# Attention output made transposed in 32-column tiles, beside the first feed-forward layer

## The chip, the core and the metric

The kernel runs on one core of a Trainium2 chip. The metric is the device time of one execution, in microseconds; the time of before is the median of 3 runs. The core's engines run unsynchronised programs and wait for each other through semaphores: PE (TensorE, the matmuls; PEld is its weight load), DVE (VectorE), ACT (ScalarE), POOL (GpSimd) and SP, which here only issues transfers.

## The reference, cut to what matters

Three things are computed one after the other: a linear attention with decay over 768 tokens (4 batches, 8 heads of 48), a gated layer of 384 -> 1536 -> 384 on all 3072 tokens, and a second layer of 384 -> 2048 -> 384.

```python
for t in range(S):                       # state: (B, H, D, D)
    kt, vt, rt = (k[:, :, t], v[:, :, t], r[:, :, t])
    cur = np.einsum('bhd,bhe->bhde', u[None] * kt, vt)
    y[:, :, t] = np.einsum('bhd,bhde->bhe', rt, state + cur)
    state = w[None, :, :, None] * state + np.einsum('bhd,bhe->bhde', kt, vt)
...
x = y as (3072, 384)
g = x @ w_gate;  x = (g * sigmoid(g) * (x @ w_val)) @ w_out
h = x @ w_in;    return (h * tanh(softplus(h))) @ w_out2
```

The term with `u` is a token's own: its output gets v times one number per head, the sum over the head of r·u·k. Below this number is called the own sum.

## The kernel before

**Tiling.** The tokens are cut into `NJ` = 6 blocks of 128; a block of 4 batches is 512 columns of the feed-forward layers. Inside a block the attention of one batch is a batch's "turns" on PE. The first layer runs in 72 units (block j, slice f of 128 of its 1536 features). A unit has 9 matmuls for the gate, 9 for the value and 9 for the previous unit's output ("out"): every product of 128x512 is three matmuls (`product`, L227 to L229), since each operand is split into a high part rounded to fp32r and the rest. ACT makes the silu (L614) and the high part of the product (`g_hi`, L620), DVE the product (L618) and the low part (`g_lo`, L626).

**Attention.** Blocks 0 and 1 (`EARLY` = 2) are done first, in the first 45 us. The attention of blocks 2 to 5 lies beside the units: the strings in `UNITS` give a unit's order and mark places ("fill"), and `Filler` hands the steps of `STEPS` out over these places. For a batch, PE has four turns: the scores k·r of 128 x 128 tokens (L444, 8 matmuls), the output as token x feature (L460 from the state, L468 from the masked scores, 24 matmuls with stationary tiles of 64 columns), three transposes of the output one place later (`at_flip`, L539), and the batch's addition to the state (L502, 8 matmuls; none in block 5). A plain fp32 matmul shows as two rows in the trace. Between them DVE masks the scores (L451, two of 128x512), adds the own term to the output (y, L489), takes the low part of the transposed output (L544), sums the state (L518) and makes the own sums (L425); ACT takes the high part (L540). POOL makes r·k (L417), times u (L419), own sum times v (L426), and puts the decay on r and k (L392, two of 128x512) and on the natural k (L434).

**Weights.** `Weights.tick` prepares one weight tile of 128x384 beside the units: ACT (L136), four DVE instructions on the bits (L144, L150, L158, L163), ACT again (L179) and one subtraction (`rest`, L185), on DVE for the first 36 tiles and on POOL after that. Units below 14 have two ticks, units 14 to 18 three in two units, 19 to 23 none, later units 1.3 each until all are done, at about 389 us. Every engine runs its instructions in program order, so a waiting instruction holds up all behind it.

Of the kernel before, what the change touches and what calls it, by code (L numbers as in the profile page):

```python
# [9 lines left out]
F32 = mybir.dt.float32  # L10
# [3 lines left out]
ALU = mybir.AluOpType  # L14
# [30 lines left out]
LAST = ["flip0", "low2"]  # L45

KEYS = [[(1, b, "mykeys0")] for b in range(B)]
STATES = [[(1, b, "state0" if i == 0 else "sum0")] for b in range(B) for i in range(2)]
NEXT = [[(1, B - 1, "own0 own1 decay1")], [(1, B - 1, "own2 decay0 keys0")]]
# [19 lines left out]
def tile_decay_attention_then_two_ffns(  # L69
    ctx: ExitStack,  # L70
    tc: tile.TileContext,
    rk_t: bass.AP,
    rkv_n: bass.AP,
    w_t: bass.AP,
    u_n: bass.AP,
    u_t: bass.AP,
# [181 lines left out]
    def at_tiles(j, b):  # L258

        if j < EARLY:  # L260
            r, k = (f32(wpool.tile([P, 2, DM], F32R, name="w_split")) for _ in range(2))
            r, k = (t.rearrange("p w n -> p (w n)")[:, : NPAIR * CH] for t in (r, k))
            r, k = (t.rearrange("p (n t) -> p n t", n=NPAIR) for t in (r, k))
            at_in[j, b] = {"r": r, "k": k}
        else:
            t = apool.tile([P, 2, NPAIR, CH], F32, name="rk_sb")
            n = apool.tile([P, 3, H, D], F32, name="n_sb")
            at_in[j, b] = {"r": t[:, 0], "k": t[:, 1], "both": t, "n": n}
            at_in[j, b].update({"av": n[:, 0], "kn": n[:, 1], "v": n[:, 2]})
# [5 lines left out]
    def load_at(j, b):  # L275
        a = at_in[j, b]
        if j < EARLY:
            nc.sync.dma_start(out=a["k"], in_=rk_t[j, b, :, 1])
            nc.sync.dma_start(out=a["r"], in_=rk_t[j, b, :, 0])
            nc.sync.dma_start(out=a["kv"], in_=rkv_n[j, b, :, 1:])  # L280
        else:
            nc.sync.dma_start(out=a["both"], in_=rk_t[j, b])
            nc.sync.dma_start(out=a["n"], in_=rkv_n[j, b])


    for b in range(B):
# [75 lines left out]
    late = apool.tile([P, 2, NPAIR, CH], F32, name="rk_sb")[:, 0]  # L362
    tabn = const.tile([P, H, D], F32, name="tabn")

    def tab_of_keys():
# [7 lines left out]
            tabn, ptab.rearrange("p n (i d) -> p (n i) d", d=PD)[:, :, 0:D], AF.Copy  # L373
        )

    mask3 = (
        mask.bitcast(mybir.dt.uint16).rearrange("p (o t) -> p o t", o=1).to_broadcast([P, NPAIR, CH])
    )


    state = const.tile([P, B, NPAIR, 2 * D], F32, name="state")
# [30 lines left out]
    def at_own(j, b, i):  # L412

        a = at_in[j, b]
        if i == 0:
            bonus[j, b] = epool.tile([P, DM], F32, name="pr").rearrange("p (h d) -> p h d", d=D)
            nc.gpsimd.tensor_tensor(out=bonus[j, b], in0=a["av"], in1=a["kn"], op=ALU.mult)  # L417
        elif i == 1:
            nc.gpsimd.tensor_tensor(  # L419
                out=bonus[j, b], in0=bonus[j, b], in1=u_sb.rearrange("p (h d) -> p h d", d=D),  # L420
                op=ALU.mult,
            )
        else:
            sums = epool.tile([P, H, 1], F32, name="bonus")
            nc.vector.reduce_sum(out=sums, in_=bonus.pop((j, b)), axis=AX.X)  # L425
            nc.gpsimd.tensor_tensor(  # L426
                out=a["av"], in0=a["v"], in1=sums.to_broadcast([P, H, D]), op=ALU.mult
            )

    def at_keys(j, b):  # L430
# [15 lines left out]
                    start=True, stop=True,  # L446
                )

    def at_mask(j, b):
        for g in range(2):  # L450
            nc.vector.copy_predicated(out=scores[g], mask=mask3, data=at[j, b]["scores"][g])  # L451

    def at_out(j, b):

        a = at[j, b]
        ps = a["out"] = ps_at.tile([P, 512], F32, name="at")
        if j:
# [15 lines left out]

    def at_mine(j, b):

        a = at[j, b]
        a["y"] = ypool.tile([P, DM], F32, name="y")
        nc.vector.tensor_tensor(
            out=a["y"].rearrange("p (h d) -> p h d", d=D), in0=a["v"],
            in1=a["sums"].rearrange("p (h o) -> p h o", o=1).to_broadcast([P, H, D]), op=ALU.mult,  # L480
        )

    def at_y(j, b):
        a = at[j, b]
        if j < EARLY:
            y = own = a["y"]
        else:
            y, own = ypool.tile([P, DM], F32, name="y"), a["av"].rearrange("p h d -> p (h d)")
        nc.vector.tensor_tensor(out=y, in0=a["out"][:, :DM], in1=own, op=ALU.add)  # L489
        a["y"] = y  # L490
# [60 lines left out]
    def after(j, b, n):  # L551
        n += j * B + b
        return order[n] if n < len(order) else None

    def at_part(j, b, part):

        nxt = after(j, b, 1)
        name, i = part[:-1], int(part[-1])
        if name == "scores":
            at_scores(j, b)  # L560
        elif name == "mask":
            at_mask(j, b)
        elif name == "out":
            at_out(j, b)
            at_fade(j, b)
        elif name == "y":
            at_y(j, b)
        elif name == "state":
            at_state(j, b)
        elif name == "sum":  # L570
            at_sum(j, b)
        elif name == "back" and b:
            at_flip(j, b - 1)
        elif name == "flip":
            at_flip(j, b)
        elif name == "low" and (i == 2 or i == 1 and b):
            at_low(j, b - (i == 1))
        elif name == "load":
            ahead = after(j, b, 2)
            if ahead:  # L580
                at_tiles(*ahead)
                load_at(*ahead)
        elif name == "own" and nxt:
            at_own(*nxt, i)
        elif name == "decay" and nxt:
            at_decay(*nxt, i)
        elif name == "keys" and nxt:
            at_keys(*nxt)
        elif name == "mykeys":
            at_keys(j, b)  # L590

    def at_steps(j):

        return [[(j, b, step)] for b in range(B) for step in STEPS + LAST * (b + 1 == B)]
# [223 lines left out]
    for f in range(NF1):  # L818
# [193 lines left out]
```

## Time and profile before

| what | value |
|---|---|
| median of 3 runs | 957.48 us (956.59 to 960.96) |
| span of the profiled execution | 955.2 us |
| PE busy | 944.3 us (99%) |
| PE weight load busy | 770.6 us (81%) |
| DVE busy | 628.2 us (66%) |
| ACT busy | 473.8 us (50%) |
| POOL busy | 163.5 us (17%) |
| granted clock of PE | full in all 40 slices |

The profiled execution's span lies 2.3 us below the median of the runs. Read it so: busy shares are means over the whole span, and what a stage waits for is read in its own stretch. A PE row lasts longer than the distance to the next row's start, since matmuls are pipelined; the distance between starts is what a matmul costs.

### The profile page before, as it was taken

The numbers are of one execution on the slowest core, as the hardware profiler recorded it, in microseconds if no ns is written. First come the engines' busy times: TensorE is split into PE (matmuls) and PEld (weight loads), VectorE is DVE, ScalarE is ACT, GpSimd is POOL, SyncE is SP. The second block draws the span as 40 slices with busy tenths as digits, with TensorE's granted clock in tenths as the row PEclk, the third lists the DMA queues.
The fourth block names the chain that finished last, engine by engine and source line by source line (L and its number), as shares of the span: only waits on it lengthen the run. The fifth ranks groups of instructions, "written<-read, shape, count | busy, mean of one in ns | idle before, by whom it ended". The sixth has DMA issues, their size and how long they took to land.

```text
span 955.2 us, 14700 instructions
## 1 busy us (share of the span) xinstructions
PE 944.3 (99%) x5707; PEld 770.6 (81%) x5707; DVE 628.2 (66%) x1170; ACT 473.8 (50%) x841; POOL 163.5 (17%) x148
## 2 busy tenths in 40 slices
PE   8999999999999999999999999999999999999998
PEld 6778888787788787888888888888888888888886
DVE  8998868446765766533322249868678777787774
ACT  2455543323343433311221248867676776777673
POOL 5100001764654464322000000000000000000000
PEclk9999999999999999999999999999999999999999
DMA  8464432446646655230046630001001010000000
GB/s 324 176 195 133 132 101 66 128 128 173 218 148 208 217 164 192 92 103 1 1 165 198 197 102 22 12 26 41 1 34 34 0 47 21 1 34 1 33 1 34
DMA packets 35781, 93.17 MB, mean 98 GB/s; under 512 B 4224, under 2 KB 4352, under 8 KB 35712
## 3 DMA queue, kind: packets, MB, share of 16 engines
q1 hardware_dynamic: 35280, 91.44, 29.5%
q0 software_dynamic: 432, 0.79, 0.6%
q8 instruction: 45, 0.74, 0.3%
q14 instruction: 24, 0.20, 0.1%
HBM read 69.41 MB, written 22.81 MB: 97 GB/s over the span
## 4 chain that ended last, share of the span: by engine, by line
PE 87%; DVE 5%; DMA 4%; issue 2%; ACT 1%; POOL 1%; SPq 0%; DVEq 0%; POOLq 0%; ACTq 0%
PE mm L227 12%; PE mm L228 11%; PE mm L229 11%; PE acc L227 11%; PE acc L228 11%; PE acc L229 11%; PE at L228 5%; PE at L229 4%; PE at L227 4%; DMA w_split<-rk_t 2%; PE at L468 2%; PE at L444 2%; PE at L460 1%; DVE w_num L150 1%; DVE w_num L144 1%
## 5 line engine op out<-in xcount | busy, mean ns | idle before, releaser
L227 PE MATMUL mm<-x_hi,w_split 128*128 128x512 f32 x546 | 217.6, 398 | 0.0
L229 PE MATMUL mm<-x_hi,w_split 128*128 128x512 f32 x546 | 213.0, 390 | 0.0
L228 PE MATMUL mm<-x_lo,w_split 128*128 128x512 f32 x546 | 212.9, 390 | 0.0
L228 PE MATMUL acc<-g_lo,w_split 128*128 128x512 f32 x483 | 188.4, 390 | 0.8 <-DVE g_lo L626 0.7
L227 PE MATMUL acc<-g_hi,w_split 128*128 128x512 f32 x483 | 188.8, 391 | 0.0
L229 PE MATMUL acc<-g_hi,w_split 128*128 128x512 f32 x483 | 188.0, 389 | 0.0
L618 DVE TENSOR_TENSOR o<-mm,o 128x512 f32<-128x512 f32 x72 | 49.7, 691 | 192.4 <-PE mm L229 162.4
L227 PEld LDWEIGHTS mm<-x_hi,w_split 128*128 128x128 f32 x546 | 102.5, 188 | 22.7 <-DVE o L618 0.4
L229 PEld LDWEIGHTS mm<-x_hi,w_split 128*128 128x128 f32 x546 | 102.5, 188 | 21.8
L228 PEld LDWEIGHTS mm<-x_lo,w_split 128*128 128x128 f32 x546 | 102.6, 188 | 20.0
L620 ACT ACTIVATE g_hi<-o 128x512 fp32r<-128x512 f32 x72 | 45.5, 632 | 141.4 <-DVE o L618 141.1
L228 PEld LDWEIGHTS acc<-g_lo,w_split 128*128 128x128 f32 x483 | 90.7, 188 | 21.0 <-DVE g_lo L626 2.0
L227 PEld LDWEIGHTS acc<-g_hi,w_split 128*128 128x128 f32 x483 | 90.6, 188 | 19.2
L229 PEld LDWEIGHTS acc<-g_hi,w_split 128*128 128x128 f32 x483 | 90.7, 188 | 18.8
L614 ACT ACTIVATE o<-mm 128x512 f32<-128x512 f32 x72 | 42.8, 594 | 89.5 <-PE mm L229 82.4
L848 ACT ACTIVATE e<-h 128x512 f32<-128x512 f32 x96 | 60.0, 626 | 53.4 <-DVE h L842 50.4
L855 ACT ACTIVATE e<-e 128x512 f32<-128x512 f32 x96 | 59.6, 621 | 49.4 <-DVE e L852 49.3
L862 DVE TENSOR_TENSOR h<-h,e 128x512 f32<-128x512 f32 x96 | 60.0, 687 | 20.5 <-ACT e L861 20.5
L185 POOL TENSOR_TENSOR w_raw<-w_num,w_raw 128x384 fp32r<-128x384 f32 x32 | 40.9, 1279 | 160.4 <-ACT w_raw L179 158.3
L227 PE MATMUL at<-x_hi,w_split 128*128 128x512 f32 x174 | 67.7, 389 | 0.0
L228 PE MATMUL at<-x_lo,w_split 128*128 128x512 f32 x174 | 67.7, 389 | 0.0
L229 PE MATMUL at<-x_hi,w_split 128*128 128x512 f32 x174 | 67.7, 389 | 0.0
(105 smaller groups left out, 1347.6 us busy)
## 6 DMA issues: line engine op xcount, KB each, us to landing
w_raw<-w SPq DMA_DIRECT2D x68, 384.0 KB, 3.5
w2s<-w_raw SPq DMA_DIRECT2D x32, 384.0 KB, 3.7
w_split<-w2s SPq DMA_DIRECT2D x32, 384.0 KB, 3.5
n_sb<-rkv_n SPq DMA_DIRECT2D x16, 576.0 KB, 4.9
rk_sb<-rk_t SPq DMA_DIRECT2D x16, 512.0 KB, 4.5
mid<-o SPq DMA_DIRECT2D x18, 256.0 KB, 2.2
rows<-mid SPq DMA_DIRECT2D x18, 256.0 KB, 2.6
y<-o SPq DMA_DIRECT2D x18, 256.0 KB, 2.3
```

The lines of the kernel that those rows point to most:

```text
L185: eng.tensor_tensor(out=t[:, 1, :], in0=num, in1=f32(t[:, 0, :]), op=ALU.subtract)
L227: nc.tensor.matmul(acc, lhsT=wt[:, 0, sl], rhs=hi, start=start, stop=False)
L228: nc.tensor.matmul(acc, lhsT=wt[:, 0, sl], rhs=lo, start=False, stop=False)
L229: nc.tensor.matmul(acc, lhsT=wt[:, 1, sl], rhs=hi, start=False, stop=stop)
L444: nc.tensor.matmul(ps[g][:, i, :], lhsT=a["k"][q, i, :], rhs=a["r"][q, i, :], start=True, stop=True,)
L468: nc.tensor.matmul(ps[t, h * D : (h + 1) * D], lhsT=scores[h % 2][:, h // 2, t], rhs=a["v"][:, h, :], start=(j == 0 and h == heads[0]), st ...
L614: nc.scalar.activation(sg, ps, AF.Silu)
L618: nc.vector.tensor_tensor(out=sg, in0=ps, in1=sg, op=ALU.mult)
L620: nc.scalar.activation(hi, sg, AF.Copy)
L848: nc.scalar.activation(es[n], hs[n], AF.Exp)
L855: nc.scalar.activation(e, e, AF.Ln, bias=1.0)
L862: nc.vector.tensor_tensor(out=hs[n], in0=hs[n], in1=es[n], op=ALU.mult)
```

## The change

**The output is made transposed.** For blocks 2 to 5 `at_turned` makes the output as feature x token at once: 28 fp32 matmuls per batch, each with a stationary tile of 32 columns (12 from the state, 16 from v) and 128 moving columns, consecutive ones on the column positions 0, 32, 64 and 96. `hi` (ACT) and `low` (DVE) read that PSUM tile. The transposes and the addition y are gone there. The own term enters as a diagonal: POOL writes the own sums on the diagonal of both score tiles (`at_diagonal`, two tensor_tensors of 128x512 over the identity), and the mask's copy then writes the scores beside it; L426 is gone.

**The steps are set anew.** A batch has two turns on PE: "out state" and "scores". POOL's steps are done two batches ahead. Block 2 begins one unit earlier, at unit 18, with its first steps (`AHEAD`, for its batches 0 and 1) put among the steps of units 14 to 17. For blocks 3 to 5 (`SPREAD`, 28 steps over 34 places) the mask of the even heads and that of the odd heads are two steps.

**A gate's low part in its own unit.** From unit 18 on `g_lo` is made by `mine`, behind the unit's own product, instead of `rest` in the next unit.

**Inputs.** r, k and v of a batch come by feature or in 32-column order in one transfer of 768 KB (`rkv_t`), and r and k by token in one of 384 KB, where there were 512 and 576 KB.

```diff
 STEPS = [
-    "scores0 own0", "mask0 back0 own1", "out0 low1 decay0 own2", "y0 state0 decay1 keys0",
-    "sum0 load0",
+    "out state load2 diag1", "hi low fade sum keys1", "scores1 first2 second2",
+    "mask1 total2 later2 sooner2",
+]
+SPREAD = [
+    "out state load2 diag1", "hi fade keys1", "low", "sum first2", "scores1 second2",
+    "even1 total2", "odd1 later2 sooner2",
 ]
...
+AHEAD = [
+    [(2, 0, "first second")], [(2, 0, "total later sooner")], [(2, 0, "diag keys")],
+    [(2, 1, "first second")], [(2, 1, "total later sooner")],
+]
+BEGIN = [[(2, 0, "scores")], [(2, 0, "mask")]]
...
     "gate rest fill act val mul tick out fill tick fill tick",
-    "gate rest fill act val mul fill tick out fill tick tick",
+    "gate rest fill act val fill mul mine tick tick out fill",
+    "gate fill act val fill mul mine out fill",
+    "gate fill act val mul tick mine fill out fill tick tick",
...
+    def at_diagonal(j, b):
+        for g in range(2):
             nc.gpsimd.tensor_tensor(
-                out=a["av"], in0=a["v"], in1=sums.to_broadcast([P, H, D]), op=ALU.mult
+                out=scores[g], in0=four(ident),
+                in1=at_in[j, b]["sums"][:, g::2, :].to_broadcast([P, NPAIR, CH]), op=ALU.mult,
             )
...
+    def at_turned(a, b, ps):
+        a["turned"] = ps
+        todo = [
+            (i, m, state[:, b, i, m * QUAD : (m + 1) * QUAD], a["r"][:, i, :])
+            for m in range(3) for i in range(NPAIR)
+        ]
+        for g, places in enumerate((((0, 0), (1, QUAD)), ((2, 2 * QUAD + PD - D), (1, QUAD + PD - D)))):
+            todo += [
+                (i, m, a["v"][i // 2][:, i % 2, c : c + QUAD], scores[g][:, i, :])
+                for m, c in places for i in range(NPAIR)
+            ]
+        ends = {(3 * i + m) % 4: n for n, (i, m, _, _) in enumerate(todo)}
+        begun_q = set()
+        for n, (i, m, lhsT, rhs) in enumerate(todo):
+            c, q = divmod(3 * i + m, 4)
+            nc.tensor.matmul(
+                ps[q * QUAD : (q + 1) * QUAD, c, :], lhsT=lhsT, rhs=rhs,
+                start=q not in begun_q, stop=ends[q] == n, skip_group_check=True,
+            )
+            begun_q.add(q)
...
     beside = {
-        2 * PAIRED: (KEYS, 3),
-        2 * PAIRED + 1: (STATES, 8),
-        ready: (NEXT + at_steps(2), 14),
+        2 * PAIRED: ([k + a for k, a in zip(KEYS, AHEAD[:1] + [[]] * 3)], 3),
+        2 * PAIRED + 1: ([STATES[i] + ([] if i % 2 else AHEAD[1 + i // 2]) for i in range(8)], 8),
+        ready - 1: (BEGIN + at_steps(2, STEPS), 18),
     }
-    beside.update({12 * j - 12: (at_steps(j), 34) for j in range(3, NJ)})
+    beside.update({12 * j - 12: (at_steps(j, SPREAD), 34) for j in range(3, NJ)})
```

PE's queue, at one batch's turns in block 2, before (`at<-state`, L460, and `at<-n_sb`, L468, are the output; L444 scores, L539 transposes of the batch ahead, L502 state):

```order
694 L229 MATMUL acc_2113<-g_hi,w_split 128x512
695 L444 MATMUL at<-rk_sb 128x128 x8
696 L539 MATMUL at<-ident,y 128x128 x3
697 L460 MATMUL at<-state,rk_sb 64x96 x8
698 L468 MATMUL at<-n_sb,s_229 64x48 x8
699 L468 MATMUL at<-n_sb,s_230 64x48 x8
700 L502 MATMUL at<-n_sb 48x48 x8
701 L227 MATMUL mm<-x_hi,w_split 128x512
```

and a batch's turn for output (L521) and state (L552) after:

```order
677 L249 MATMUL mm<-x_hi,w_split 128x512
678 L521 MATMUL at<-rkv_sb,state 32x128 x12
679 L521 MATMUL at<-s_229,rkv_sb 32x128 x8
680 L521 MATMUL at<-s_230,rkv_sb 32x128 x8
681 L552 MATMUL at<-rkv_sb,n_sb 48x48 x8
682 L247 MATMUL mm<-x_hi,w_split 128x512
```

The 24 matmuls of 64 columns and the 3 transposes became 28 matmuls of 32 columns; the scores stand in another place, between other matmuls of the layer.

POOL's queue, at the first work for block 2, before (L399 belongs to the early keys, L185 is a weight's `rest`, the first on POOL):

```order
19 L434 TENSOR_TENSOR w_split<-w_split,tabn 128x384
20 L399 TENSOR_TENSOR pr<-w_split 128x512 x4
21 L185 TENSOR_TENSOR w_raw<-w_num,w_raw 128x384
22 L417 TENSOR_TENSOR pr<-n_sb 128x384
23 L419 TENSOR_TENSOR pr<-pr,u_sb 128x384
24 L392 TENSOR_TENSOR rk_sb<-rk_sb,tab 128x512
```

and after (L422 are the early keys; L440 and L442 are r·k and times u, L415 the decay, L453 the diagonal, L462 the decayed keys, L205 the first `rest` on POOL):

```order
19 L462 TENSOR_TENSOR w_split<-w_split,tabn 128x384
20 L422 TENSOR_TENSOR pr<-w_split 128x512 x4
21 L440 TENSOR_TENSOR pr<-n_sb 128x384
22 L442 TENSOR_TENSOR pr<-pr,u_sb 128x384
23 L415 TENSOR_TENSOR rkv_sb<-rkv_sb,tab 128x512 x2
24 L453 TENSOR_TENSOR s_229<-ident,bonus 128x512
25 L453 TENSOR_TENSOR s_230<-ident,bonus 128x512
26 L462 TENSOR_TENSOR n_sb<-n_sb,tabn 128x384
27 L440 TENSOR_TENSOR pr<-n_sb 128x384
28 L442 TENSOR_TENSOR pr<-pr,u_sb 128x384
29 L415 TENSOR_TENSOR rkv_sb<-rkv_sb,tab 128x512 x2
30 L205 TENSOR_TENSOR w_raw<-w_num,w_raw 128x384
```

The work for block 2's batches 0 and 1 moved from behind that `rest` to before it.

DVE's queue in block 3 at the masks of batch 1, before (L618 product, L451 the two masks, L144 to L163 a tick, L648 a copy of the layer's output):

```order
330 L618 TENSOR_TENSOR o<-mm,o 128x512
331 L451 COPY_PREDICATED s_229<-mask,at 128x512
332 L451 COPY_PREDICATED s_230<-mask,at 128x512
333 L144 TENSOR_SCALAR w_num<-w_num 128x384
334 L150 SCALAR_TENSOR_TENSOR w_num<-w_raw,w_num 128x384
335 L158 TENSOR_SCALAR w_num<-w_num 128x384
336 L163 SCALAR_TENSOR_TENSOR w_num<-w_raw,w_num 128x384
```

and after (L663 product, L164 to L183 a tick, L671 `g_lo`, L479 the masks, L448 the own sums):

```order
348 L479 COPY_PREDICATED s_229<-mask,at 128x512
349 L448 TENSOR_REDUCE bonus<-pr 128x8
350 L663 TENSOR_TENSOR o<-mm,o 128x512
351 L164 TENSOR_SCALAR w_num<-w_num 128x384
352 L170 SCALAR_TENSOR_TENSOR w_num<-w_raw,w_num 128x384
353 L178 TENSOR_SCALAR w_num<-w_num 128x384
354 L183 SCALAR_TENSOR_TENSOR w_num<-w_raw,w_num 128x384
355 L671 TENSOR_TENSOR g_lo<-o,g_hi 128x512
356 L479 COPY_PREDICATED s_230<-mask,at 128x512
357 L663 TENSOR_TENSOR o<-mm,o 128x512
```

The second mask moved behind the unit's product, a tick and `g_lo`.

## Rows read from the trace of the kernel before

**Rows 1.** The page, part 1: busy us and share of each engine, instructions.
```profile
PE 944.3 (99%) x5707; PEld 770.6 (81%) x5707; DVE 628.2 (66%) x1170; ACT 473.8 (50%) x841; POOL 163.5 (17%) x148
```
**Rows 2.** PE's waits, 130 to 476 us: line, releaser, us, times, longest.
```profile
PE at L460 <- DVE s L451: 1.6, 4, 0.5
PE acc L228 <- DVE g_lo L626: 0.7, 1, 0.7
PE at L444 <- POOL rk_sb L392: 0.4, 1, 0.4
```
**Rows 3.** Timeline of PE, 231 to 248 us: start, duration, instruction, count.
```profile
232.03 1.16 PE L444 MATMUL at<-rk_sb 48*128 48x128 f32 x16
233.12 0.51 PE L227 MATMUL acc<-g_hi,w_split 128*128 128x512 f32 x1
...
238.35 0.49 PE L539 MATMUL at<-ident,y 128*128 128x128 f32 x3
238.60 0.48 PE L227 MATMUL mm<-x_hi,w_split 128*128 128x512 f32 x1
...
240.84 0.88 PE L460 MATMUL at<-state,rk_sb 128*64 128x96 f32 x16
241.56 1.09 PE L468 MATMUL at<-n_sb,s 128*64 128x48 f32 x32
242.57 0.50 PE L227 MATMUL acc<-g_hi,w_split 128*128 128x512 f32 x1
...
246.33 0.39 PE L228 MATMUL mm<-x_lo,w_split 128*128 128x512 f32 x1
246.56 0.39 PE L229 MATMUL mm<-x_hi,w_split 128*128 128x512 f32 x1
246.88 0.56 PE L502 MATMUL at<-n_sb 128*48 128x48 f32 x16
247.37 0.50 PE L227 MATMUL mm<-x_hi,w_split 128*128 128x512 f32 x1
```
**Rows 4.** Groups of POOL by line, 130 to 476 us: busy us, mean ns.
```profile
L392 POOL TENSOR_TENSOR rk_sb<-rk_sb,tab 128x512 f32<-128x512 f32 x32 | 45.9, 1442 | 0.0
```
**Rows 5.** Timeline of POOL, then DVE, 255 to 261 us.
```profile
257.62 1.02 POOL L419 TENSOR_TENSOR pr<-pr,u_sb 128x384 f32<-128x384 f32 x1
258.60 1.41 POOL L392 TENSOR_TENSOR rk_sb<-rk_sb,tab 128x512 f32<-128x512 f32 x1
...
257.86 1.00 DVE L144 TENSOR_SCALAR w_num<-w_num 128x384 f32<-128x384 f32 x1
258.79 1.65 DVE L150 SCALAR_TENSOR_TENSOR w_num<-w_raw,w_num 128x384 uint32<-128x384 uint32 x1
260.36 0.35 DVE L158 TENSOR_SCALAR w_num<-w_num 128x384 uint32<-128x384 uint32 x1
260.62 0.55 DVE L163 SCALAR_TENSOR_TENSOR w_num<-w_raw,w_num 128x384 uint32<-128x384 uint32 x1
261.09 1.33 DVE L451 COPY_PREDICATED s<-mask,at 128x512 f32<-128x512 uint16 x2
```
**Rows 6.** Timeline of POOL, then DVE, 253 us.
```profile
253.35 2.31 POOL L185 TENSOR_TENSOR w_raw<-w_num,w_raw 128x384 fp32r<-128x384 f32 x1 [4.39 <-ACT w_raw L179]
...
254.11 0.68 DVE L626 TENSOR_TENSOR g_lo<-o,g_hi 128x512 fp32r<-128x512 f32 x1
```
**Rows 7.** Windows: stretch, length, busy us of PE, PEld, DVE, ACT, POOL.
```profile
44.00:130.00 86.00, 85.38 (x400) 69.88 (x396) 75.11 (x177) 46.05 (x90) 0.00 (x0) 1.00 0.51 158
130.00:175.00 45.00, 44.62 (x313) 35.78 (x312) 33.02 (x66) 17.05 (x34) 11.14 (x11) 1.00 0.26 81
```
**Rows 8.** Timeline of PE, 60 us: a wait in the stretch without POOL.
```profile
61.06 0.50 PE L228 MATMUL at<-g_lo,w_split 128*128 128x512 f32 x1 [0.62 <-DVE g_lo L626]
```
**Rows 9.** Timeline of DVE: the product and `g_lo` at 141 and 151 us.
```profile
141.50 0.69 DVE L618 TENSOR_TENSOR o<-mm,o 128x512 f32<-128x512 f32 x1 [2.06 <-PE mm L229]
151.64 0.69 DVE L626 TENSOR_TENSOR g_lo<-o,g_hi 128x512 fp32r<-128x512 f32 x1
```

More of the change, by code (lines that the diff above doesn't have):

```diff
@@ L28 @@
 HALF = CH // 2
+WIDE = NPAIR * CH
+VH = NPAIR * PD
+ROW = WIDE + VH
+QUAD = 32
 GUARD = 20.0
@@ L41 @@
 STEPS = [
-    "scores0 own0", "mask0 back0 own1", "out0 low1 decay0 own2", "y0 state0 decay1 keys0",
-    "sum0 load0",
-]
[L45 to L49, printed above, removed]
+    "out state load2 diag1", "hi low fade sum keys1", "scores1 first2 second2",
+    "mask1 total2 later2 sooner2",
+]
+SPREAD = [
+    "out state load2 diag1", "hi fade keys1", "low", "sum first2", "scores1 second2",
+    "even1 total2", "odd1 later2 sooner2",
+]
+KEYS = [[(1, b, "keys")] for b in range(B)]
+STATES = [[(1, b, "state" if i == 0 else "sum")] for b in range(B) for i in range(2)]
+AHEAD = [
[3 more added lines that the diff above has]
+BEGIN = [[(2, 0, "scores")], [(2, 0, "mask")]]
 UNITS = [
@@ L72, in tile_decay_attention_then_two_ffns @@
     rk_t: bass.AP,
-    rkv_n: bass.AP,
+    kv_n: bass.AP,
+    rkv_t: bass.AP,
+    rk_n: bass.AP,
     w_t: bass.AP,
@@ L265, in at_tiles @@
         else:
[L266 to L269, printed above, removed]
+            t = apool.tile([P, 2, ROW], F32, name="rkv_sb")
+            n = apool.tile([P, 2, H, D], F32, name="n_sb")
+            r, k = (t[:, i, :WIDE].rearrange("p (n t) -> p n t", n=NPAIR) for i in range(2))
+            v = [t[:, i, WIDE:].rearrange("p (n c) -> p n c", n=2) for i in range(2)]
+            at_in[j, b] = {"r": r, "k": k, "v": v, "both": t, "n": n, "rn": n[:, 0], "kn": n[:, 1]}
     def at_natural(j, b):
@@ L279, in load_at @@
             nc.sync.dma_start(out=a["r"], in_=rk_t[j, b, :, 0])
-            nc.sync.dma_start(out=a["kv"], in_=rkv_n[j, b, :, 1:])
+            nc.sync.dma_start(out=a["kv"], in_=kv_n[j, b])
         else:
-            nc.sync.dma_start(out=a["both"], in_=rk_t[j, b])
-            nc.sync.dma_start(out=a["n"], in_=rkv_n[j, b])
+            nc.sync.dma_start(out=a["both"], in_=rkv_t[j - EARLY, b])
+            nc.sync.dma_start(out=a["n"], in_=rk_n[j - EARLY, b])
     for b in range(B):
@@ L360, in tile_decay_attention_then_two_ffns @@
     nc.vector.tensor_tensor(out=w128, in0=pw[:, :, HALF], in1=pw[:, :, HALF], op=ALU.mult)
-    late = apool.tile([P, 2, NPAIR, CH], F32, name="rk_sb")[:, 0]
+    late = apool.tile([P, 2, ROW], F32, name="rkv_sb")[:, 0, :WIDE]
+    late = late.rearrange("p (n t) -> p n t", n=NPAIR)
     tabn = const.tile([P, H, D], F32, name="tabn")
@@ L374, in tab_of_keys, with four @@
         )
-    mask3 = (
-        mask.bitcast(mybir.dt.uint16).rearrange("p (o t) -> p o t", o=1).to_broadcast([P, NPAIR, CH])
-    )
+    def four(t):
+        return t.rearrange("p (o t) -> p o t", o=1).to_broadcast([P, NPAIR, CH])
+    mask3 = four(mask.bitcast(mybir.dt.uint16))
     state = const.tile([P, B, NPAIR, 2 * D], F32, name="state")
@@ L423, in at_own @@
         else:
-            sums = epool.tile([P, H, 1], F32, name="bonus")
-            nc.vector.reduce_sum(out=sums, in_=bonus.pop((j, b)), axis=AX.X)
+            a["sums"] = epool.tile([P, H, 1], F32, name="bonus")
+            nc.vector.reduce_sum(out=a["sums"], in_=bonus.pop((j, b)), axis=AX.X)
+    def at_diagonal(j, b):
+        for g in range(2):
             nc.gpsimd.tensor_tensor(
-                out=a["av"], in0=a["v"], in1=sums.to_broadcast([P, H, D]), op=ALU.mult
+                out=scores[g], in0=four(ident),
+                in1=at_in[j, b]["sums"][:, g::2, :].to_broadcast([P, NPAIR, CH]), op=ALU.mult,
             )
@@ L447, in at_scores, with at_mask @@
                 )
-    def at_mask(j, b):
-        for g in range(2):
+    def at_mask(j, b, gs=range(2)):
+        for g in gs:
             nc.vector.copy_predicated(out=scores[g], mask=mask3, data=at[j, b]["scores"][g])
@@ L456, in at_out @@
         ps = a["out"] = ps_at.tile([P, 512], F32, name="at")
+        if j >= EARLY:
+            return at_turned(a, b, ps[:, :DM].rearrange("p (c t) -> p c t", c=KC))
         if j:
@@ L484, in at_y @@
         a = at[j, b]
[L485 to L490, printed above, removed]
+        nc.vector.tensor_tensor(out=a["y"], in0=a["out"][:, :DM], in1=a["y"], op=ALU.add)
     def at_state(j, b):
@@ L543, in at_low @@
         hi, lo = xs[j, "x"]
+        a = at.pop((j, b))
         nc.vector.tensor_tensor(
-            out=lo[:, :, cols(b)], in0=at.pop((j, b))["flip"], in1=f32(hi[:, :, cols(b)]),
+            out=lo[:, :, cols(b)], in0=a["flip" if j < EARLY else "turned"], in1=f32(hi[:, :, cols(b)]),
             op=ALU.subtract,
@@ L553, in after, with at_steps @@
         return order[n] if n < len(order) else None
-    def at_part(j, b, part):
[L557 to L594, printed above, removed]
+    PARTS = {
+        "out": at_out,
+        "state": at_state,
+        "sum": at_sum,
+        "fade": at_fade,
+        "hi": at_flip,
+        "low": at_low,
+        "keys": at_keys,
+        "scores": at_scores,
+        "mask": at_mask,
+        "even": lambda j, b: at_mask(j, b, [0]),
+        "odd": lambda j, b: at_mask(j, b, [1]),
+        "diag": at_diagonal,
+        "load": lambda j, b: (at_tiles(j, b), load_at(j, b)),
+        "first": lambda j, b: at_own(j, b, 0),
+        "second": lambda j, b: at_own(j, b, 1),
+        "total": lambda j, b: at_own(j, b, 2),
+        "sooner": lambda j, b: at_decay(j, b, 0),
+        "later": lambda j, b: at_decay(j, b, 1),
+    }
+    def at_part(j, b, part):
+        name = part.rstrip("12")
+        to = after(j, b, int(part[len(name) :] or 0))
+        if to:
+            PARTS[name](*to)
+    def at_steps(j, steps):
+        return [[(j, b, step)] for b in range(B) for step in steps]
     def do(step):
@@ L743, in unit1 @@
         gate = val = act = None
-        for part in UNITS[n if n < 2 else 2 if n < 2 * PAIRED else 3 if n < 24 else 4].split():
+        form = n if n < 2 else 2 if n < 2 * PAIRED else 3 if n < ready - 1 else 4 if n < ready else 5
+        for part in UNITS[form if n < 24 else 6].split():
             if part == "gate":
@@ L756, in unit1 @@
                 ffn1_rest(*units[n - 1][:2], nc.vector)
+            elif part == "mine":
+                ffn1_rest(j, f, nc.vector)
             elif part == "out" and n:
@@ L981, in tiles_out @@
         return a.reshape(-1, P, KC, P).transpose(1, 0, 2, 3)
+    rkv_t = np.concatenate(
+        [
+            np.stack([by_feature(r), by_feature(k)], axis=3).reshape(NJ, B, P, 2, WIDE),
+            pad(by_token(v), 4).reshape(NJ, B, P, 2, VH),
+        ],
+        axis=4,
+    )
     arrays = {
[L984 to L985 removed]
+        "rk_t": rkv_t[:EARLY, ..., :WIDE].reshape(EARLY, B, P, 2, NPAIR, CH),
+        "kv_n": np.stack([by_token(k), by_token(v)], axis=3)[:EARLY],
+        "rkv_t": rkv_t[EARLY:],
+        "rk_n": np.stack([by_token(r), by_token(k)], axis=3)[EARLY:],
         "w_t": w_t.reshape(P, NPAIR),
```

14 lines of the change are left out of this document (8 added, 6 removed).

## The prediction

> **What bounds the kernel now.** I read the shares first: PE is busy 944.3 of 955.2 us, DVE 628, POOL 163.5 [rows 1]. So PE sets the time, and an edit counts by the PE time it takes out or by the waits it puts before PE. Then PE's waits in the stretch that holds the attention of blocks 2 to 5: three kinds, 2.7 us in all [rows 2]. The old kernel therefore hides nearly everything DVE and POOL do; what they gain is worth nothing, what they lose can show. Third, PE's timeline, for the price of a batch's turns [rows 3]. Last, the rows of DVE and POOL where both work at once, since the change moves work between and along these two [rows 4 to 7].
>
> **What a batch costs PE before.** Two matmuls of the layer start 0.23 us apart (246.33, 246.56), and a turn enters 0.32 after the last of them, 0.09 more than a matmul would take [rows 3]. Scores: 233.12 - 232.03 = 1.09, with the entry 1.18. Output: 242.57 - 240.84 = 1.73, with the entry 1.82. State: 247.37 - 246.88 = 0.49, with the entry 0.58. Transposes: 0.25. The first matmul behind each turn lasts 0.50 or so where others last 0.39, so 0.11 more for each of the four. Sum: 3.83 + 0.44 = 4.27 us; 3.58 in block 5, which makes no state.
>
> **What it costs after.** Scores stay. The output is 28 fp32 matmuls, 56 rows, each with 128 moving columns. Its price hangs on how many column positions run side by side, and no row here has more than two. The 16 rows of L460 take 241.56 - 240.84 = 0.72, so a pair of 96 columns costs 0.09 and one of 128 would cost 0.12; the scores bear that out with 8 pairs in 1.09 less an exit of about 0.13. Four side by side: 14 groups x 0.12 = 1.68. Two: 28 x 0.12 = 3.36. The weight loads set a floor: L468 with 64-column weights and 48 moving columns puts 32 rows into 242.57 - 241.56 = 1.01, 0.032 a row, and 56 rows at that pace are 1.77. A tile of 64 columns is half of the array and two of them run abreast, so I take four quarters abreast, 1.68 (for a range of 1.68 to 3.36). With entry 0.09 and exit 0.13 the turn is 1.90; with the state joined on, 1.90 - 0.13 + 0.09 + 0.49 = 2.35, where I count a change of tile shape like an entry.
>
> By the Trainium skill's TensorEngine Tiling (Array Packing), section Tiling Modes, a 128x32 shape is four independent tiles, which is the value I took; its TensorE: Matmul & The Clock Gate, Part 3, gives 2.38 times for three column tiles instead of 3; with that ratio as an estimate a batch would pay 1.68 x 3 / 2.38 = 2.12, 0.44 more, near rival 3's price. No run here shows either.
>
> Sum after: 2.35 + 1.18 + 2 x 0.11 = 3.75 per batch, 3.30 in block 5. So blocks 3 and 4 gain 8 x 0.52 = 4.2, block 5 4 x 0.28 = 1.1. In block 2 the four kinds already stand in one turn in PE's order, so two turns save only the transposes and pay an entry more: 4 x 0.1 = 0.4. In all 5.7 us.
>
> **Waits that go.** L460's 1.6 and L444's 0.4 belong to the old places, and the 0.7 of L228 is a `g_lo` held up behind the next unit's start, which `mine` moves ahead [rows 2]. Best case -2.7; with 5.7 that is -8.4. Removing y (DVE) and L426 (POOL) takes nothing from PE by itself: DVE was 66% busy.
>
> **What DVE and POOL do to each other.** At 257.62 to 260.01 two POOL instructions of 2.43 us run; in that time DVE's L144 lasts 1.00 instead of 0.35 and L150 1.65 instead of 0.55 [rows 5], 1.75 lost, 0.72 of POOL's time. The opposite also stands there: at 253.35 a POOL instruction lasts 2.31, to 255.66, and DVE is at its last instruction of a row without gaps, which ends 254.79 [rows 6]. So either engine holds the other out, and the loss is POOL's when DVE is first. I take 0.72 of POOL's time as DVE's loss, with 0 as the other end. By the Trainium skill's SBUF — State Buffer, Who interferes with whom, the two engines share a port pair under a lock and the first to issue blocks the other; the trace agrees with 1.00 against 0.35.
>
> **New waits.** POOL now pays two 128x512 diagonals for one L426, at 1.44 each like L392 [rows 4].
>
> (a) The start. POOL had nothing to do from 44 to 130 us, 0 instructions [rows 7], since its queue stood behind the first `rest`; now four instructions for block 2's first batch run as soon as their inputs land, at about 49 us: 2 x 1.02 + 2 x 1.44 = 4.9 us. DVE has no gap there, and at 61.06 PE already waits for `g_lo` [rows 8], so DVE's loss goes straight to PE: 4.9 x 0.72 = 3.5 (0 to 4.9).
>
> (b) Units 15 to 17. Diagonal, keys, and the second batch's first steps: 4 x 1.44 + 3 x 1.02 = 8.8 of POOL, 6.3 of DVE. DVE is busy 33.02 of 45 us there [rows 7], and from 141.50 to 151.64, between that product and that `g_lo`, it has hardly a gap [rows 9]. What falls there waits on PE, what falls later doesn't: 4 (0 to 6.3).
>
> (c) Blocks 3 and 4 from their first batch to the second. The order of DVE puts the odd heads' mask behind product, tick and `g_lo`. Alone that is 0.69 + (0.26 + 0.47) x 2 + 0.68 + 0.67 = 3.5 us [rows 5, 6], a mask being half of the 1.33 for two, from 0.39 after the value's last matmul starts: ready at 3.9. PE has nine matmuls of the output, 2.07, one interval and entry more, 0.32, and the first 20 of the turn's 28, 10 x 0.12: 3.6. A stall of 0.3 bare, 2.1 with one encounter as in rows 5, 3.9 with two; POOL has both decays and a weight's `rest` to do there. I take 2.5 for each block, 5 (0.6 to 8).
>
> (d) Elsewhere. POOL has 1.8 us more per batch, 1.3 of DVE, less the 0.5 of y that is gone: 16 x 0.8 = 13 us more for DVE, in stretches where it is a quarter to a third idle. 2 (0 to 6).
>
> Sum of new waits: 3.5 + 4 + 5 + 2 = 14.5. Net -8.4 + 14.5 = +6.1 on the span. The profiled span is 955.2 and the median of the runs 957.48, 2.3 above; put on the median that is 963.6, and I say 963.0, since waits in a row cover each other a little.
>
> The transfers: 1152 KB per batch for 1088, on a queue of SP that nothing on PE waited for [rows 2]; nothing, and half a us a batch if an input came late. `at_turned` and ACT's read of it stand off PE's path.
>
> **Rivals.**
> 1. **DVE keeps POOL out.** If, as at 253.35, POOL does the waiting, (a) to (d) shrink to the bare 0.6 and little more, say 1, and the gain stays: 957.5 - 8.4 + 1 = 950. For it: rows 6, and idle time of DVE. Against: rows 5, and POOL's queue has more to do with less slack. This is the faster side; it decides if DVE's loss falls below a quarter of POOL's time.
> 2. **Two abreast only.** 1.68 more for 16 batches, 27 us; the longer turns cover about half of the new waits: 957.5 - 8.4 + 27 + 6 = 982. For it: every row here shows two. Against: 96 and 128 columns cost by columns, not by rows.
> 3. **Three abreast.** If the fourth position doesn't overlap with the others, 56 rows go in threes: 18.7 x 0.12 = 2.24, 0.56 more for 16 batches, 9 us, on the forecast: 972. For it: no row shows more than two. Against: as in rival 2.
> 4. **Even.** Gain whole and about 8 of the 14.5 us: 957. Rows 2 speak for it: the old kernel hid similar work. The ends of (a) to (d) are far apart.
>
> **How the numbers follow.** Forecast 0.40, going from 958 to 968 (three fifths of that over +0.5%). Rival 1: 0.18. Rival 2: 0.10. Rival 3: 0.12. Rival 4: 0.20. About 0.5%, 4.8 us, is what a measurement of this kernel can tell from no change. Faster (below 952.7): 0.18. Slower (above 962.3): 0.25 + 0.10 + 0.12 = 0.47. Same: the rest, 0.35. The range goes from 949, rival 1's time less 1, to 977, which leaves out rival 2 and half of rival 1's lower tail.
>
> **What would show it.** In the changed trace: the turn at L521 with the state takes 2.35 from its first row to the layer's next matmul less 0.1 (3.4 and more: rival 2); its rows start in groups of four. DVE's groups between 48 and 62 us have bit instructions over 0.9 us, and PE waits for `g_lo` there for 3 us more than 0.6. PE's list of waits names L671's `g_lo` and, before L521, the mask L479, over 10 us together; if it names less than 4, the contention is mis-sized and the result is rival 1 or 4. It is all wrong if an input's transfer, or the high part on ACT, stands in that list.

## The result, and the profile after

The changed kernel takes 968.5 us (median of 4, 964.5 to 971.8) where the kernel before takes 958.07 (956.59 to 960.96) beside it: 1.0106 times, 95% interval 1.0073 to 1.0138. Slower, as forecast, and by more than the 963.0 that was said.

The profiled execution has a span of 969.8 us, 14.6 over that of before. The page's first part, to be read against [rows 1]:

```profile
PE 949.0 (98%) x5787; PEld 772.9 (80%) x5787; DVE 635.5 (66%) x1154; ACT 473.7 (49%) x841; POOL 180.1 (19%) x164
PEclk8899999999999999999999999999999999999999
```

PE is busy 4.7 us longer although its turns cost less, and the second line shows one reason: in the first two of forty slices its granted clock was not full. PE's waits between 44 and 476 us (line, what it waited for, us in all, times, longest), to be read against [rows 2, 8]:

```profile
PE mm L247 <- DVE o L663: 3.7, 1, 3.7
PE acc L248 <- DVE g_lo L671: 3.7, 1, 3.7
PE at L521 <- DVE s L479: 3.0, 2, 2.7
PE mm L247 <- ACT o L659: 2.2, 1, 2.2
```

(Left out is a wait of 0.4 that belongs to the early blocks.) The four are 12.6 us where before had 3.3, and each is one place in the kernel, at 63, 164, 258 and 246 us; 0.3 of the third lies at 347.

**The turn.** PE's timeline at a batch's turn for output and state, to be read against [rows 3]:

```profile
279.09 0.39 PE L249 MATMUL acc<-g_hi,w_split 128*128 128x512 f32 x1
279.41 0.86 PE L521 MATMUL at<-rkv_sb,state 128*32 128x128 f32 x24
280.08 1.06 PE L521 MATMUL at<-s,rkv_sb 128*32 128x128 f32 x32
281.07 0.56 PE L552 MATMUL at<-rkv_sb,n_sb 128*48 128x48 f32 x16
281.57 0.50 PE L247 MATMUL mm<-x_hi,w_split 128*128 128x512 f32 x1
```

24 rows in 280.08 - 279.41 = 0.67: six groups of four at 0.11. The turn costs 281.57 - 279.09 - 0.23 = 2.25 us. The gain that the change was priced with is there.

**The start, 57 to 63 us.** DVE, then POOL, then PE:

```profile
56.91 1.37 DVE L170 SCALAR_TENSOR_TENSOR w_num<-w_raw,w_num 128x384 uint32<-128x384 uint32 x1
58.21 1.37 DVE L205 TENSOR_TENSOR w_split<-w_num,w_split 128x384 fp32r<-128x384 f32 x1
59.50 1.42 DVE L178 TENSOR_SCALAR w_num<-w_num 128x384 uint32<-128x384 uint32 x1
60.84 1.61 DVE L183 SCALAR_TENSOR_TENSOR w_num<-w_raw,w_num 128x384 uint32<-128x384 uint32 x1
62.38 0.68 DVE L663 TENSOR_TENSOR o<-mm,o 128x512 f32<-128x512 f32 x1
...
56.66 1.22 POOL L440 TENSOR_TENSOR pr<-n_sb 128x384 f32<-128x384 f32 x1 [12.49 <-DMA n_sb<-rk_n]
57.95 1.21 POOL L442 TENSOR_TENSOR pr<-pr,u_sb 128x384 f32<-128x384 f32 x1
59.13 2.91 POOL L415 TENSOR_TENSOR rkv_sb<-rkv_sb,tab 128x512 f32<-128x512 f32 x2
...
63.11 0.80 PE L247 MATMUL mm<-x_hi,w_split 128*128 128x512 f32 x1 [3.74 <-DVE o L663]
64.12 0.63 PE L249 MATMUL mm<-x_hi,w_split 128*128 128x512 f32 x1
66.55 0.40 PE L249 MATMUL mm<-x_hi,w_split 128*128 128x512 f32 x1
```

Four POOL instructions of 5.3 us, and the four DVE instructions beside them last 1.37, 1.37, 1.42 and 1.61 instead of 0.55, 0.55, 0.35 and 0.55: DVE does one of its own for one of POOL's. The product (L663) comes when POOL is done, PE waits 3.74 for it. Behind the wait PE's rows last 0.63 and start 0.43 apart: eight steps from 63.11 to 66.55 take 3.44 where 8 x 0.23 = 1.84 were to be expected, so the lower of the two clock levels costs 1.6 on top. The same stands at 164 us (1.5) and at 246 (1.6), 4.7 in all.

**The first 45 us.** Windows: stretch, length, busy us of PE, PEld, DVE, ACT, POOL, granted clock; first after, then the kernel with another order of masks (below), whose first 45 us hold the same code:

```profile
12.00:32.00 20.00, 18.43 (x242) 15.08 (x243) 14.22 (x23) 3.42 (x9) 7.29 (x7) 0.58 0.92 349
```
```profile
12.00:32.00 20.00, 18.58 (x384) 15.45 (x382) 19.64 (x33) 6.22 (x18) 10.58 (x9) 1.00 0.92 349
```

From 12 to 32 us the granted clock averaged 0.58 in after and 1.00 in the other. The first matmul of unit 0 starts at 52.59 in after and at 44.75 in before: 7.8 of the 14.6 us lie ahead of all that the change touches in the units. The other kernel starts unit 0 at 44.89 with the same code ahead of it, so the code does not force this loss; how often it comes was not settled. From there to the end it is 917.2 against 910.45, **6.8 us more**: 9.3 of waits, 4.7 of clock behind waits, and 7.2 less for all the rest, which I put down to the turns.

### The profile page after: what moved, and what is told of

It reads as the page before. It is cut to its first block, busy times and chain, and to the rows that moved or that the text cites. A ratio compares the mean times of both kernels' runs of the same rounds, so it can differ in the third digit from the quotient of the medians.

```text
span 969.8 us, 14841 instructions
## 1 busy us (share of the span) xinstructions
PE 949.0 (98%) x5787; PEld 772.9 (80%) x5787; DVE 635.5 (66%) x1154; ACT 473.7 (49%) x841; POOL 180.1 (19%) x164
## 4 chain that ended last, share of the span: by engine, by line
PE 72%; ACT 1%; DVE 1%; issue 0%
PE acc L247 10%; PE acc L248 10%; PE acc L249 10%; PE mm L247 9%; PE mm L248 9%; PE mm L249 9%; PE at L249 4%; PE at L248 4%; PE at L247 4%; PE at L521 2%; PE at L472 1%; PE at L552 0%; ACT e L908 0%; DVE g_lo L671 0%; DVE s L479 0%
## 5 line engine op out<-in xcount | busy, mean ns | idle before, releaser
L663 DVE TENSOR_TENSOR o<-mm,o 128x512 f32<-128x512 f32 x72 | 49.8, 691 | 179.4 <-PE mm L249 143.1
L671 DVE TENSOR_TENSOR g_lo<-o,g_hi 128x512 fp32r<-128x512 f32 x72 | 56.1, 780 | 22.4 <-ACT g_hi L665 22.3
```

Source lines behind the costliest of these rows:

```text
L663: nc.vector.tensor_tensor(out=sg, in0=ps, in1=sg, op=ALU.mult)
L671: eng.tensor_tensor(out=lo, in0=sg, in1=f32(hi), op=ALU.subtract)
```

## Experiments

**The four POOL instructions alone, in the kernel before.**

```diff
-NEXT = [[(1, B - 1, "own0 own1 decay1")], [(1, B - 1, "own2 decay0 keys0")]]
+NEXT = [[(1, B - 1, "own2 keys0")]]
...
+    for i in range(2):
+        at_own(2, 0, i)
+    at_decay(2, 0, 1)
+    at_decay(2, 0, 0)
     ready = NF1 + PAIRED
```

> The kernel before with one part of the change alone: POOL's r times k, times u, and the decays for block 2's first batch are queued before POOL's first weight subtraction instead of behind it; PE, DVE, ACT and the loads are as before. Theory: these four instructions run at about 50 to 55 us in DVE's row without gaps, DVE loses 3.5 us, PE waits 3 to 4 us more for g_lo at 55 to 62, with 1 to 2 us of lower clock behind it, and wins back about 0.5 us at block 2's start: 4 us more than before, ratio 1.004. Rival (POOL waits for DVE): ratio 1.000 or a little less.

960.43 us, 1.0021 (1.0002 to 1.0041). DVE, POOL and PE:

```profile
50.04 1.37 DVE L150 SCALAR_TENSOR_TENSOR w_num<-w_raw,w_num 128x384 uint32<-128x384 uint32 x1
51.34 1.63 DVE L185 TENSOR_TENSOR w_split<-w_num,w_split 128x384 fp32r<-128x384 f32 x1
...
50.95 3.14 POOL L392 TENSOR_TENSOR rk_sb<-rk_sb,tab 128x512 f32<-128x512 f32 x2
...
55.43 0.80 PE L227 MATMUL mm<-x_hi,w_split 128*128 128x512 f32 x1 [3.33 <-DVE o L618]
```

One part of the change, with none of its new turns, transfers or units, makes the wait at the start: 3.33 us, where before has 0.62 [rows 8]. The median rose by 1.8 and not 4, but its interval goes from 0.2 to 3.9 us. In the profiled execution the stretch from unit 0 on takes 914.1 against 910.45, 3.7 more: PE's waits are 4.3 against 3.3, since two of before's four waits for masks and the 0.7 for `g_lo` at block 3 are gone (L460 waits 0.8 where it waited 1.6), and behind the wait of 3.33 the granted clock is 0.57 from 54 to 62 us, 3.4 lost (a window as above):

```profile
54.00:62.00 8.00, 6.57 (x18) 5.26 (x19) 8.00 (x20) 4.69 (x9) 0.09 (x1) 0.57 0.45 130
```

The rival, POOL waiting for DVE, would have left the start as it was.

**The loads of block 2's first two batches at unit 13,** so that POOL's work finds a DVE with time to spare.

```diff
-    for b in range(2):
-        at_tiles(EARLY, b)
-        load_at(EARLY, b)
+    LATE = {13: 0}
...
     for n in range(len(units) - NF1):
+        if n in LATE:
+            for b in range(2) if True else [LATE[n]]:
+                at_tiles(EARLY, b)
+                load_at(EARLY, b)
```

> The changed kernel with the two input loads of block 2's batches 0 and 1 issued at unit 13 instead of before unit 0, so that POOL's four instructions for batch 0 land at about 140 us, where DVE is 2.3 of 5 us busy, and not at 56.66. My theory (DVE starved by POOL at 57 to 62 us causes PE's wait of 3.74 at 63.11, and the lower clock behind it costs 1.6): the wait at 63 falls below 0.7, the granted clock stays full there, the time is 5 us (0.5%) below the changed kernel, ratio to before about 1.005. Rival (the start is slow for another reason, the larger transfer of 768 KB or the copy order): the wait stays over 3 us, ratio about 1.011.

962.55 us, 1.0052 (1.0024 to 1.0081). PE's waits from 44 to 476 us:

```profile
PE at L521 <- DVE s L479: 5.2, 2, 4.9
PE acc L248 <- DVE g_lo L671: 3.7, 1, 3.7
PE mm L247 <- ACT o L659: 1.5, 1, 1.5
PE at L248 <- DVE g_lo L671: 0.6, 1, 0.6
```

The wait at the start is back at 0.6 and the ratio is the one expected. The POOL instructions now run at 130 us, slow DVE just as much there (L170 lasts 1.38, L205 1.64), and nobody waits. Two other waits stayed, and the one for the mask grew from 2.7 to 4.9, with 3.4 of lower clock behind it (granted clock 0.57 from 250 to 258 us). So in the profiled executions the stretch from unit 0 on is only 1.7 below after's (915.5 against 917.2); that the ratio of the medians came out as expected is partly chance.

**The second batch's load at unit 17, and its POOL steps in unit 18.**

```diff
-    [(2, 1, "first second")], [(2, 1, "total later sooner")],
 ]
-BEGIN = [[(2, 0, "scores")], [(2, 0, "mask")]]
+BEGIN = [
+    [(2, 0, "scores"), (2, 1, "first second")], [(2, 0, "mask"), (2, 1, "total later sooner")],
+]
...
+    LATE = {13: 0, 17: 1}
...
-        2 * PAIRED + 1: ([STATES[i] + ([] if i % 2 else AHEAD[1 + i // 2]) for i in range(8)], 8),
+        2 * PAIRED + 1: ([STATES[i] + ([] if i % 2 or i > 2 else AHEAD[1 + i // 2]) for i in range(8)], 8),
...
+        if n in LATE:
+            for b in range(2) if False else [LATE[n]]:
+                at_tiles(EARLY, b)
+                load_at(EARLY, b)
```

> As the run before, but the second batch's load comes at unit 17 and its POOL steps in unit 18, so that POOL has 3 us of work and not 8.2 beside DVE at 152 to 160 us. Theory: the wait of 3.68 for g_lo at 164 falls below 1 and the clock stays full there, 4 to 5 us less than the run with late loads alone, ratio to before about 1.000. Rival (the wait at 164 comes from PE's new order of states and units or from DVE's own queue): it stays over 2.5 us, ratio 1.005.

957.96 us, 1.0011 (0.9985 to 1.0037). The wait of 3.7 for `g_lo` is no longer in the list:

```profile
PE at L522 <- DVE s L480: 5.2, 2, 4.9
PE mm L248 <- ACT o L660: 2.0, 1, 2.0
```

Beside these two stands only the 0.6 of the start. So the burst of POOL beside DVE at 152 to 160 us was the cause at 164, and not PE's order of states or DVE's own queue. In after that burst reads so, POOL and then DVE:

```profile
153.99 1.02 POOL L462 TENSOR_TENSOR n_sb<-n_sb,tabn 128x384 f32<-128x384 f32 x1
154.96 1.13 POOL L440 TENSOR_TENSOR pr<-n_sb 128x384 f32<-128x384 f32 x1
156.17 1.20 POOL L442 TENSOR_TENSOR pr<-pr,u_sb 128x384 f32<-128x384 f32 x1
157.34 2.97 POOL L415 TENSOR_TENSOR rkv_sb<-rkv_sb,tab 128x512 f32<-128x512 f32 x2
...
154.04 1.19 DVE L164 TENSOR_SCALAR w_num<-w_num 128x384 f32<-128x384 f32 x1
155.16 1.35 DVE L170 SCALAR_TENSOR_TENSOR w_num<-w_raw,w_num 128x384 uint32<-128x384 uint32 x1
159.09 1.64 DVE L183 SCALAR_TENSOR_TENSOR w_num<-w_raw,w_num 128x384 uint32<-128x384 uint32 x1
```

**The odd heads' mask ahead of the tick,** alone in after, and on top of the split loads.

```diff
-    "gate fill act val mul tick mine fill out fill tick tick",
+    "gate fill act val mul fill tick mine out fill tick tick",
```

> The changed kernel with one edit: in the units from 24 on the second place stands before the tick and g_lo and not behind them, so the odd heads' mask follows the product on DVE. Theory: the wait of 2.69 at 258 us inside the output turn falls below 0.5, that of 0.29 at 347 goes, the waits at 63, 164 and 246 stay; 2 to 3 us less than the changed kernel, ratio about 1.008. Rival (g_lo, now later, takes its place): a wait for g_lo of 1 us or more turns up behind these turns and the ratio stays at 1.011.

967.85 us, 1.0094 (1.006 to 1.0127), an interval that holds both 1.008 and 1.011. Half held: the wait inside the turn fell from 2.7 to 0.4. But a wait of 2.9 appeared at 305.76, for ACT, which stood before a weight tile's first instruction until its load had landed; SP had issued nothing between 297.20 and 303.37. ACT, then SP:

```profile
304.27 0.54 ACT L156 ACTIVATE w_num<-w_raw 128x384 f32<-128x384 f32 x1 [5.98 <-DMA w_raw<-w]
...
297.20 0.35 SPq L212 DMA_DIRECT2D w2s<-w_raw  x1
303.37 0.33 SPq L145 DMA_DIRECT2D w_raw<-w  x1
```

The rival (`g_lo` too late) did not come; what took the place was a third thing that neither had named.

> Late loads split by batch, as in the run that came out at 1.0011, with the odd heads' mask ahead of the tick from unit 24 on. Theory: the wait of 4.9 at 245 falls below 0.5; 4 to 6 us less, ratio 0.995. Rival, from the run with that edit alone: a wait of 2.9 for ACT behind a late weight load turns up at the next change of block and takes half of it back, ratio 0.999.

956.18 us, 0.9981 (0.9957 to 1.0005), between the two. The mask's wait went from 5.2 to 2.2 in all, not under 0.5; the waits for ACT rose from 2.0 to 4.4. Of these 1.6, at 293 us, are what the rival named: ACT stood 4.7 us before a late weight tile. The other 2.9, at block 1's output, are the old wait of 2.0 grown longer.

**Both masks in one step, a place earlier,** on the split loads.

```diff
-    "even1 total2", "odd1 later2 sooner2",
+    "mask1 total2", "later2 sooner2",
```

> Late loads split by batch, and both masks in one step of blocks 3 to 5, where only the even heads' stood, with the order of ticks as in the changed kernel. Theory: s_230 is ready a place earlier, the wait of 4.9 at 245 falls below 1, no new wait at the change of block since the ticks keep their places; ratio 0.994. Rival: the masks wait on PE's scores at that place and hold up g_lo on DVE; a wait for g_lo of 1 us or more takes its place, ratio 0.999.

953.01 us, 0.9948 (0.9929 to 0.9968). No wait for a mask is left in blocks 2 to 5, and no new one of more than 0.5 for `g_lo`; the wait for ACT at block 1's output is 3.2 where it was 2.0. It is the order that the kernel before had, with both masks right behind each other.

```profile
PE mm L248 <- ACT o L660: 3.2, 1, 3.2
PE acc L249 <- DVE g_lo L672: 0.5, 1, 0.5
```

Behind that wait of 3.2, which ends at 238.09, the granted clock stayed full:

```profile
238.00:246.00 8.00, 7.91 (x83) 6.46 (x83) 7.93 (x15) 3.65 (x9) 3.35 (x4) 1.00 0.67 218
```

**A fourth buffer for the silu and the outputs,** on top of that (its room is taken from tiles used only at the start).

```diff
-    opool = ctx.enter_context(tc.tile_pool(name="opool", bufs=3))
+    opool = ctx.enter_context(tc.tile_pool(name="opool", bufs=4))
```

> As the run with both masks early, with a fourth buffer for the tiles that hold the silu and a block's output (the room for it comes from tiles used only at the start). Theory: the wait of 2.0 for ACT at 232, where the silu waits for a buffer until the transfer of block 1's output has landed, goes and with it about 1.6 of lower clock; 3 us less than that run, ratio 0.991. Rival (the wait comes from ACT's queue, not from a buffer): the same time as that run.

950.12 us, 0.9912 (0.9882 to 0.9941): the wait for the silu is gone, and this version is faster than both kernels, 18 us below the changed one. Its interval overlaps that of the run before, so that the buffer did it rests on the list of waits. The 1.6 of lower clock in the expectation were not there to be won: that run had none behind the wait. A wait of 1.4 for `g_lo` is new:

```profile
PE acc L249 <- DVE g_lo L672: 1.4, 1, 1.4
```

**The turn's matmuls in another order,** those on one column position behind each other.

```diff
+        todo[:12] = sorted(todo[:12], key=lambda e: ((3 * e[0] + e[1]) % 4))
+        todo[12:20] = sorted(todo[12:20], key=lambda e: ((3 * e[0] + e[1]) % 4))
+        todo[20:] = sorted(todo[20:], key=lambda e: ((3 * e[0] + e[1]) % 4))
```

> The changed kernel with the 28 matmuls of an output turn in another order: those on one column position one after another, so that neighbours seldom are on different positions. Theory (the gain in the turn comes from four column positions abreast): the rows of a turn no longer start in groups of four, an output and state turn takes 2 to 4 us instead of 2.2 more than its matmuls' neighbours, and the whole is 30 us or more above the changed kernel, near 1000. Rival (32-column tiles are cheap in any order): the turn stays within 0.3 us and the time near 968.

One run: 979.15 us. The turn:

```profile
279.85 0.39 PE L249 MATMUL acc<-g_hi,w_split 128*128 128x512 f32 x1
280.17 1.26 PE L524 MATMUL at<-rkv_sb,state 128*32 128x128 f32 x20
281.16 0.31 PE L524 MATMUL at<-s,rkv_sb 128*32 128x128 f32 x2
281.23 0.30 PE L524 MATMUL at<-rkv_sb,state 128*32 128x128 f32 x2
...
282.56 0.56 PE L555 MATMUL at<-rkv_sb,n_sb 128*48 128x48 f32 x16
283.05 0.50 PE L247 MATMUL mm<-x_hi,w_split 128*128 128x512 f32 x1
```

283.05 - 279.85 - 0.23 = 2.97 us instead of 2.25: 0.72 for 16 batches, 11.5 us, and this run is 10.7 above after's median. The order of positions has a price, as it must if the positions run abreast; but the price is far below the 30 us expected. Rows of the masked scores, which the program puts behind all rows of the state, start among these (281.16 before 281.23): PE starts matmuls for one position ahead of earlier ones for another. That the other had to be busy for this was not tested.

## Why the prediction was right, and where it was off

It was right in direction, and in mechanism for the waits (a) to (c) and for the turns. That the sums agree, +6.8 us on the stretch from unit 0 on for +6.1 forecast, is partly luck: turns and waits alone come to 9.3 - 7.2 = +2.1, which is nearer to rival 4 than to the forecast, and 4.7 us of lower clock behind the waits, for which the prediction had no term, make up the rest. Point by point:

- **The turns.** Output and state 2.25, forecast 2.35; four positions abreast, as taken. Rivals 2 and 3 fall. The whole gain is about 7.2 by difference, forecast 5.7; where the 1.5 more come from is not shown. Other kernels give the same difference. Take from the stretch from unit 0 to the end PE's waits and what the granted clock lost: the split loads leave 910.9 - 7.8 - 3.4 = 899.7, the version with the fourth buffer 901.8 - 2.0 - 0 = 899.8, after 917.2 - 12.6 - 4.7 = 899.9, and before 910.45 - 3.3 = 907.15.
- **(a) the start.** A wait of 3.74 in place of 0.62, so 3.1 more; forecast 3.5. PE waited for the product and not, as forecast, for `g_lo`, which stands behind it on DVE. Shown by the kernel before with these instructions alone, and by the late loads.
- **(b) units 15 to 17.** 3.67, forecast 4. Shown by the split loads.
- **(c) the masks.** 2.7 in block 3 and 0.3 in block 4, 3.0 in all; forecast 2.5 in each, 5. The wait in block 3 sits where it was put, with three POOL instructions in DVE's chain; in block 4 none met the chain, and the 0.3 there is the bare stall that the prediction worked out. With the split loads the wait in block 3 is 4.9:

```profile
258.43 0.65 PE L521 MATMUL at<-s,rkv_sb 128*32 128x128 f32 x16 [2.69 <-DVE s L479]
```
```profile
244.82 1.08 PE L522 MATMUL at<-s,rkv_sb 128*32 128x128 f32 x16 [4.91 <-DVE s L480]
```

  There too three POOL instructions met the chain, and from the product's start to the mask's end it took 6.4 us for after's 5.8. Most of the difference is PE's: from the matmul behind the wait for ACT to the turn it took 6.3 us there and 8.0 in after, where part of it ran at the lower clock. So PE came earlier and waited longer.
- **(d) elsewhere.** No wait, forecast 2.
- **Old waits.** Gone, as forecast in the best case.
- **Not in the sum.** First, 2.2 us at 246: the silu waits for a buffer that a transfer of block 1's output still reads. In before ACT waited too, and PE did not. ACT of before, then ACT and PE of after:

```profile
226.91 0.60 ACT L614 ACTIVATE o<-mm 128x512 f32<-128x512 f32 x1 [3.27 <-DMA mid<-o]
```
```profile
245.80 0.60 ACT L659 ACTIVATE o<-mm 128x512 f32<-128x512 f32 x1 [5.77 <-DMA mid<-o]
246.45 0.50 PE L247 MATMUL mm<-x_hi,w_split 128*128 128x512 f32 x1 [2.21 <-ACT o L659]
```

  From the end of block 1's output to the matmul that needs the silu, PE had 8.8 us of work in before, 2.4 of them two attention turns, and 7.5 in after, with 1.2 for one: 1.3 less cover. And from the same point the silu came 9.2 us later instead of 7.8, mostly since the transfer took longer to land (7.0 us from issue by the median, 6.1 in before); why is not shown. That the buffer makes the wait is shown by the fourth buffer. The prediction had no line for this chain. Second, 4.7 us of lower clock behind the three longest waits outside a turn. Before had no wait over 0.8 from unit 0 on and so no row of this. What the sum had too much in (c) and (d), 4.0, and too little here, 6.9, cancel in part.
- **The signs.** The turn and DVE's stretched rows came as said. The waits for `g_lo` and for the mask, which were to be over 10 us together, are 6.7, and 10.4 with the one for the product. No input's transfer and no high part stands in the list.
- **The rest of the 10 us** between the medians is not the mechanism argued about, and its cause stays open. In the profiled execution 7.8 us lie in the first 45, at a lower clock, and another kernel with the same start did not have that. Nor is the 6.8 a fixed number: that other kernel, with another order of masks and 13.4 us of waits, takes 922.0 from unit 0 to the end, 11.6 more than before, because there the lower clock cost 10 us and not 5. How often the clock falls with each kernel was not settled; the kernel before has spread too (956.45 to 964.56 in another set).

Rival 1, POOL waiting for DVE, falls: in each of the stretches shown DVE's instructions were stretched while POOL's kept 1.0 to 1.6. Rows 6 of before show the other order, in which POOL came upon a DVE that was already in a row without gaps; but POOL with several instructions in a row takes every second place. By the Trainium skill's SBUF — State Buffer, Who interferes with whom, it is issue order that decides who blocks; the alternation at 57 to 62 us agrees, with 1.4 to 1.6 for each DVE instruction. Rival 4 falls by the time, but only with the lower clock: by its waits and turns it was the nearest.

## What to carry to other kernels

Before work is moved to an earlier place in an engine's queue, look at what else runs where its inputs land, not where it is needed: five microseconds of POOL work cost PE 3.1 more of waiting beside a DVE without gaps, and none at 130 us, where DVE had time to make it up. A change that moves PE's turns can take away the cover of a chain that used to end under them, as here of a buffer's transfer, so each such chain gets a line in the sum, and so does the lower clock that can follow a wait. When the gain is in the trace and the time is not, list PE's waits by place and undo them one at a time: here four small edits (two of when loads and POOL's steps come, one of a mask's place, one of a buffer) turned +1.1% into -0.9%.

## What the runs showed of the hardware

- Four column positions of 32 run abreast: in a turn the rows of a group of four start within 0.02 us of each other, and the groups follow 0.11 us apart at 128 moving columns, where the estimate from pairs in [rows 3] was 0.12. In an order that puts one position's matmuls together they still overlap in part (2.97 against 2.25 us a turn), and rows start out of the program's order.
- Beside a POOL tensor_tensor, DVE's bit instructions, with one SBUF input or two, and its subtractions of two SBUF inputs are held up by about a POOL instruction each (0.55 becomes up to 1.65, `g_lo` 0.69 up to 1.53). The product with one input in PSUM (L663) kept 0.69 in all 16 rows of after that ran beside one.
- What a wait of PE costs in clock is no fixed price. In after waits of 2.2 to 3.7 us were followed by a stretch at the lower level that cost 1.5 to 1.6 each. By the granted clock of other runs 3.4 were lost behind 3.3 (the four POOL instructions alone) and behind each 3.7 (the masks' order alone), and nothing behind 2.0, 2.9 and 3.2 (the split loads and the two mask orders on top of them). Inside a turn nothing was lost behind 2.7 in after, 1.7 behind the same wait in the run with another order of matmuls, and 3.4 behind 4.9 with the late loads. What decides between these was not tested.
